# Rows of the experts gathered in quarters and turned by VectorE's 32x32 blocks instead of by TensorE

## The chip, the cores and the metric

The kernel runs on one core of one Trainium2 chip. The metric is the device time of one execution in microseconds (us), lower is better. One execution is also taken with the hardware profiler: its record (the trace) holds every instruction of the five engines, which are TensorE (PE, its weight loads apart as PEld), VectorE (DVE), ScalarE (ACT), GpSimd (POOL) and the queue processor SyncE (SP), and every DMA. Line numbers such as L1196 are those of the kernel before; in rows of the changed kernel they are its own.

## The reference: attention over a window, then one expert for each row

```python
def reference(q, k, v, w_gate, w_local, w1, w2):       # q, k, v: (8, 8, 576, 64)
    rel = pos[:, None] - pos[None, :]
    scores = where((rel >= 0) & (rel < 64), q @ k.T / 8, -1e9)
    x = (softmax(scores) @ v).transpose(0, 2, 1, 3).reshape(8, 576, 512)
    logits = x @ w_gate                                # 8 experts
    local = sigmoid(x @ w_local)
    for b in range(8):
        for s in range(576):
            fresh = argmax(logits[b, s])
            e = fresh if s == 0 or local[b, s] < 0.5 else prev
            prev = e
            p = softmax(logits[b, s])
            out[b, s] = p[e] * (relu(x[b, s] @ w1[e]) @ w2[e])   # w1: 512x1024, w2: 1024x512
```

## The kernel before: attention, a router and blocks of rows by expert

**Stages.** `attention` computes the 4608 rows of x in nine chunks of 512 and writes them to a table `xs` in DRAM, one row of 528 numbers for each row of x: 512 of x, and the row's weight p[e] sixteen times behind them (`Router.weigh`, L890). The `Router` finds each row's expert and sorts the rows by expert; `Router.table` (L945) makes the list of row numbers for every slot of 128 rows (`gx` to gather, `idx` to scatter) by small matmuls, once for the first three blocks during attention and once for the rest (`second`) while the first blocks run. Then `Experts.run` (L1474) works through 24 blocks, each of rows of one expert.

**Blocks.** A big block has two slots of 128 rows, a single (S) one, a half (H) 64 rows, a quarter (Q) 32 rows. `order` (L1498) is fixed: three first blocks (-1, -2, -3), then big 0, 1, S, 2, Q, 3, S, 4, 5, S, 6, Q, 7, S, 8, 9, H, 10, 11, 12, H. Big blocks are named by their number below. For a block, `rows` (L1144) issues one indirect DMA of GpSimd for each slot (128 row numbers, 128 rows of 2112 bytes), `weights` (L1170) loads 2 MB of w1 and 2 MB of w2 through SP's queue into a ring of four buffers. `turn` (L1189) makes x^T: four TensorE transposes of 128x128 into PSUM for each slot (L1196) and one copy to SBUF (L1197, VectorE in the blocks after the first three). A big block's two products are made by seven block products each instead of eight (`big_hidden` L1249, `big_result` L1302), from sums and differences that VectorE makes: of x^T and w1 in `prepare` (L1205: four of 128x256, four of 128x1024), of w2 in `prepare2` (L1238, four of 128x1024), of h in `halves` (L1243, four of 128x512).

**Order.** From the third block on, PE, SP, DVE and ACT issue in the order of the program text (`manual_schedule`); GpSimd's instructions are placed by the scheduler of the framework. In the text, iteration i issues: the gathers and weight loads of block i+2 (`fetch`), the hidden product of block i, `turn` and `prepare` of block i+1, the result of block i. On VectorE the three sums that finish y (L1327, "puts") therefore stand behind `turn` and `prepare` of the next block. The seventh product of a result reuses the PSUM buffer px that the second put reads. Two scatters per big block (L1394; the halves of its rows, y0 and y1) end it. A scatter waits until the scatter before it has landed, since both write `out`; y has two buffers, x six.

**A quarter** has its small products inside the result of the big block before it, and the block after it is turned and prepared in hooks of that result (L1550 to L1554).

Of the kernel before, what the change touches and what calls it, by code (L numbers as in the profile page):

```python
# [19 lines left out]
P = 128  # L20
# [15 lines left out]
PITCH = D + 16  # L36
# [6 lines left out]
FB = 3  # L43
# [40 lines left out]
def kernel(  # L84
# [12 lines left out]
    w1: bass.AP,  # L97
    w2: bass.AP,
# [7 lines left out]
    xs = dram.tile([N + 2, PITCH], F32, name="xs")  # L106
# [4 lines left out]
                gx=const.tile([P, NS], U32, name="gx"), gx1=const.tile([P, FIRST], U32, name="gx1"))  # L111
# [9 lines left out]
    moe = xs, w1, w2, out, tabs, lt, ident  # L121
    with ExitStack() as fast:
        ring = fast.enter_context(tc.tile_pool(name="ring", bufs=4))
        rt = Router(fast, tc, lt, xs, tabs, ident)
        ex = Experts(fast, tc, ring, *moe)
        zeros, n = ex.xp.tile([P, PITCH], F32, name="xg"), (ZR - T1) // HF
        nc.vector.memset(zeros[:HF], 0.0)
        for i in (ZR, N + 1):
            nc.gpsimd.dma_start(out=xs[i:i + 1, :], in_=zeros[:1])
        nc.gpsimd.dma_start(out=xs[T1:ZR, D:].rearrange("(c p) o -> p c o", p=HF),  # L130
                            in_=zeros[:HF, :n * (PITCH - D)].rearrange("p (c o) -> p c o", c=n))
        attention(tc, ring, kq, v3, v4, vt, vh, xs, lt, ok, wgs, wg2s, ident, rt, ex)
        ex.run(fast, rt, lambda ps: flag(nc, ps, ok, bad, tabs["ej"][:, NBLK:], rare, ident))
    if_rare = nc.values_load(rare[0:1, 0:1], min_val=0, max_val=1,  # L134
                             skip_runtime_bounds_check_because="the larger of two comparisons")
    with tc.If(if_rare > 0):
        if_bad = nc.values_load(bad[0:1, 0:1], min_val=0, max_val=1,
                                skip_runtime_bounds_check_because="the result of a comparison")
        with tc.If(if_bad > 0):
            careful(tc, q, k, v, xs, lt, wgs, ident)  # L140
# [27 lines left out]
def attention(ctx, tc, ring, kq, v3, v4, vt, vh, xs, lt, ok, wg, wg2, ident, rt, ex):  # L168
# [302 lines left out]
    for i, (sc, hp) in enumerate(units):  # L471
# [53 lines left out]
        if (sc, hp) == (NSC - 3, 3):  # L525
            ex.jobs = [ex.weights({}, -1, ("w1",), lambda: until(2, allr[:1, sc, hp, 0, :1]))]
            if side == ():
                ex.rows(ex.jobs[0], -1)
# [3 lines left out]
        if hp == HP - 1:  # L532
            if sc in GATED:
                nc.vector.tensor_reduce(lt[:, 4 * sc:4 * sc + 4, :], g.rearrange("p c h j e -> p c e (h j)"),
                                        axis=AX.X, op=Alu.add)
            nc.gpsimd.dma_start(out=xs[row_of(sc * SC):row_of(sc * SC) + SC, :D].rearrange("(c p) d -> p c d", p=P),
                                in_=x.rearrange("p c h j d -> p c (h j d)"))
# [11 lines left out]
def careful(ctx, tc, q, k, v, xs, lt, wgs, ident):  # L549
# [107 lines left out]
    def rows(st):  # L657
# [7 lines left out]
        nc.gpsimd.dma_start(out=xs[row_of(c * P):row_of(c * P) + P, :D], in_=x)  # L665
# [36 lines left out]
class Router:  # L702
# [9 lines left out]
    def __init__(self, ctx, tc, lt, xs, tabs, ident):  # L712
        self.nc, self.lt, self.xs, self.tabs, self.ident = tc.nc, lt, xs, tabs, ident
# [8 lines left out]
    def prepare(self):  # L722
# [17 lines left out]
        begin2 = tl("begin2", P, C)  # L740
# [4 lines left out]
        self.oh, self.rank = tl("oh", P, CV, E), tl("rank", P, CV, E)  # L745

# [5 lines left out]
        self.at = iota("posp", [P, 1], [[0, 1]], 1)  # L752
        self.cnt = [tl("cnt0", P, E), tl("cnt1", P, E)]
# [5 lines left out]
    def iota(self, name, shape, pattern, mul=0, base=0):  # L759
        i = self.tl(name + "_i", *shape, dt=I32)  # L760
        self.nc.gpsimd.iota(i, pattern=pattern, base=base, channel_multiplier=mul)
        f = self.tl(name, *shape)
        self.nc.vector.tensor_copy(f, i)
        return f
# [9 lines left out]
    def gate(self, part, psum):  # L774
# [111 lines left out]
        self.pt = tl("ptw", P, CMAX, PITCH - D)[:, :n]  # L886
        wide = [P, n, PITCH - D]
        vec.tensor_tensor(self.pt, last(pt).to_broadcast(wide), last(sm).to_broadcast(wide), op=Alu.mult)

    def weigh(self, part):  # L890

        chunks, xs = PART[part], self.xs
        c = chunks.start
        for a, b in ((0, T1), ) if not part else ((T1, ZR), (ZR, N)):
            for a, b in ((a, -(-a // P) * P), (-(-a // P) * P, b // P * P), (b // P * P, b)):
                if a >= b:
# [3 lines left out]
                    out=xs[row_of(a):row_of(a) + b - a, D:].rearrange("(c p) o -> p c o", p=p),  # L900
# [44 lines left out]
    def table(self, psum, cs, ns, lo, hi, idx, gx):  # L945

        nc, last, vec = self.nc, self.last, self.nc.vector
# [42 lines left out]
        else:  # L990
            vec.scalar_tensor_tensor(gx, at, float(ZR), at, Alu.is_ge, Alu.add)
# [139 lines left out]
class Experts:  # L1131


    def __init__(self, ctx, tc, ring, xs, w1, w2, out, tabs, lt, ident):
        self.tc, self.nc, self.ring = tc, tc.nc, ring
        self.xs, self.w1, self.w2, self.out, self.tabs, self.ident = xs, w1, w2, out, tabs, ident
        self.xp = ctx.enter_context(tc.tile_pool(name="ex_x", bufs=2))
        self.jobs = []
# [5 lines left out]
    def rows(self, st, n):  # L1144
# [13 lines left out]
        elif n >= KINDS[1]:  # L1158
            st.update(half=n - KINDS[1], rows=HF)
        for s in slots:  # L1160
            x = (self.xp if n == -1 else self.xq).tile([P, PITCH], F32, name="xg")
            asked = self.nc.gpsimd.indirect_dma_start(  # L1162
                out=x, out_offset=None, in_=self.xs[:rows, :],
                in_offset=bass.IndirectOffsetOnAxis(ap=gx[:, s:s + 1], axis=0))
            st["x"].append(x)
            st["asked"] = asked
        st["pw"] = [x[:, D:D + 1] for x in st["x"]]
        return st

    def weights(self, st, n, names=("w1", "w2"), behind=lambda: None):  # L1170
# [4 lines left out]
        for name, w, a, b in (("w1", self.w1, DK, F), ("w2", self.w2, FK, D)):  # L1175
# [13 lines left out]
    def turn(self, st, quiet, later=False):  # L1189
# [3 lines left out]
        for i, x in enumerate(st["x"]):  # L1193
            tp = self.ps_t.tile([P, DK, P], F32, name="tp")
            for kk in range(DK):
                nc.tensor.transpose(tp[:, kk, :n], x[a, kk * P:(kk + 1) * P], self.ident[a, a])  # L1196
            (nc.scalar.copy if quiet else nc.vector.tensor_copy)(xt[:, :, i * P:i * P + n], tp[:, :, :n])  # L1197
        if n < P:
            st["pw"] = pw = self.wk.tile([P, 1], F32, name="pw")
            for i in range(P // n):  # L1200
                nc.vector.tensor_copy(pw[i * n:(i + 1) * n], x[a, D:D + 1])
# [272 lines left out]
    def run(self, ctx, rt, last=None):  # L1474
# [44 lines left out]
        for i, n in enumerate(order):  # L1519
            quiet = i < FB  # L1520
            if i == FB - 1:
# [97 lines left out]
```

## Time and profile before

| | |
|---|---|
| time, median of 3 runs | 642.59 us (640.96 to 642.63) |
| the profiled execution | 642.1 us, of which the trace's span is 640.0 us |
| granted TensorE clock, mean | 0.994 |
| attention and router, to the first expert block | about 131 us (first transposes of L1196 at 131.2) |
| expert blocks | from there to the end |
| bytes moved by DMA | 166.43 MB, mean 260 GB/s |

The page gives busy time of each engine, a strip of the span in 40 slices, and groups of instructions by line. For this case the timeline, with the time at which each instruction starts and what ended the idle time ahead of it, says more: one block of the tail lasts 25 us, and the averages mix blocks of four kinds. Where a group stands with a mean duration, the time that one instruction takes from PE in a row of equal ones is shorter, since matmuls overlap; it is read from the start of the group to the start of the next.

### The profile page before, as it was taken

The page shows a single profiled execution, that of the slowest core. Times are in us where ns is not written, and L with a number is a line of the kernel's source. Part 1 is how long each engine was busy: PE and PEld are TensorE (multiplying, and loading weights), DVE is VectorE, ACT ScalarE, POOL GpSimd, SP SyncE. Part 2 cuts the span into 40 slices and gives each one's busy share as a digit, 9 for nine tenths or more (in the row PEclk, how much of TensorE's full clock was granted, in tenths as well). Part 3 has the DMA queues.
Part 4 walks back from the last instruction along what each step waited for, and adds up shares of the span by engine and source line. Part 5 has one row for each costly group of instructions (what it writes and reads, how often), then busy time and mean ns, then how long its engine had stood idle before and what let it go on. Part 6 is the DMA issues. An engine that isn't in the chain of part 4 may idle for free. (4 is left out here: it accounts for less than half of the span.)

```text
span 640.0 us, 14994 instructions
## 1 busy us (share of the span) xinstructions
PE 615.6 (96%) x6367; PEld 544.2 (85%) x6367; DVE 402.3 (63%) x752; ACT 200.6 (31%) x368; POOL 133.1 (21%) x132
## 2 busy tenths in 40 slices
PE   8889998899999999999999999999999999999995
PEld 7777777788889999978997999887997998899994
DVE  6676588879968775273654683362917752886730
ACT  3766765612572122113120312021211221213120
POOL 5422112430103202120302120211312022111101
PEclk9999998999999999999999999999999999999998
DMA  9999996969757645786958665769768556956501
GB/s 338 416 418 406 385 366 241 348 236 337 237 171 246 244 166 198 242 316 236 387 189 291 218 234 212 259 235 367 263 228 324 185 199 232 379 167 225 209 17 38
DMA packets 29318, 166.43 MB, mean 260 GB/s; under 512 B 8451, under 2 KB 9497, under 8 KB 20026
## 3 DMA queue, kind: packets, MB, share of 16 engines
q1 hardware_dynamic: 20394, 135.54, 58.4%
q0 software_dynamic: 8848, 29.85, 12.2%
q8 instruction: 52, 0.85, 0.5%
q14 instruction: 24, 0.20, 0.1%
HBM read 146.18 MB, written 19.59 MB: 259 GB/s over the span
## 5 line engine op out<-in xcount | busy, mean ns | idle before, releaser
L1394 POOL DMA_INDIRECT out_dram<-y,idx x36 | 41.1, 1141 | 339.1 <-DVE y L1327 196.5
L1318 PE MATMUL hp<-ws,hs 128*128 128x256 f32 x384 | 88.7, 380 | 0.0
L1318 PEld LDWEIGHTS hp<-ws,hs 128*128 128x128 f32 x384 | 72.6, 190 | 10.5 <-issue 0.8
L1268 PE MATMUL hp<-xs,ws 128*128 128x128 f32 x672 | 79.6, 275 | 0.0
L1268 PEld LDWEIGHTS hp<-xs,ws 128*128 128x128 f32 x672 | 77.3, 192 | 0.0
L1327 DVE SCALAR_TENSOR_TENSOR y<-hp,xg,kept 128x256 f32<-128x256 f32 x48 | 22.6, 482 | 74.2 <-issue 47.0
L1414 PE MATMUL hp<-xt,w 128*64 128x64 f32 (+2 forms) x640 | 66.2, 276 | 0.0
L1414 PEld LDWEIGHTS hp<-xt,w 128*128 128x128 f32 (+1 forms) x640 | 60.8, 170 | 4.1 <-issue 0.7
L1318 PE MATMUL hp<-w,h 128*128 128x256 f32 x256 | 61.1, 382 | 0.0
L1162 POOL DMA_INDIRECT xg<-xs,gx x40 | 50.3, 1258 | 45.6 <-issue 37.4
L1279 DVE TENSOR_TENSOR h<-hp,keep 128x512 f32<-128x512 f32 x42 | 28.6, 690 | 48.1 <-PE hp L1268 48.0
L1268 PEld LDWEIGHTS hp<-xt,w 128*128 128x128 f32 x448 | 53.2, 192 | 2.7 <-issue 1.3
L1268 PE MATMUL hp<-xt,w 128*128 128x128 f32 x448 | 54.7, 275 | 0.0
L1318 PEld LDWEIGHTS hp<-w,h 128*128 128x128 f32 x256 | 47.2, 190 | 6.3 <-issue 0.4
L431 PE MATMUL xo<-vb,p 128*64 128x74 f32 (+1 forms) x576 | 44.5, 230 | 7.0 <-issue 2.9
L416 ACT ACTIVATE p<-sp 128x512 f32<-128x512 f32 x72 | 39.2, 595 | 38.0 <-PE sp L385 35.9
L385 PEld LDWEIGHTS sp<-w 64*64 64x64 f32 x1296 | 38.7, 138 | 12.1 <-issue 8.5
L421 DVE TENSOR_TENSOR p<-p,mask 128x1024 f32<-128x1024 f32 x29 | 36.1, 1245 | 19.5 <-ACT p L416 19.3
L431 PEld LDWEIGHTS xo<-vb,p 128*64 128x64 f32 x576 | 38.9, 138 | 9.9 <-issue 4.4
L385 PE MATMUL sp<-w 64*64 64x128 f32 (+1 forms) x1296 | 43.8, 270 | 2.6 <-issue 1.5
L431 PE MATMUL xo<-va,p 128*64 128x74 f32 (+1 forms) x576 | 44.5, 230 | 1.2 <-issue 1.2
L1280 ACT ACTIVATE h<-h 128x512 f32<-128x512 f32 x42 | 26.3, 630 | 59.1 <-DVE h L1279 59.1
(280 smaller groups left out, 955.0 us busy)
## 6 DMA issues: line engine op xcount, KB each, us to landing
w<-in_w_dram SPq DMA_DIRECT2D x42, 2048.0 KB, 9.2
w<-in_kq_dram SPq DMA_DIRECT2D x17, 1024.0 KB, 8.7
w<-in_w_dram SPq DMA_DIRECT2D x24, 512.0 KB, 9.3
xs<-x POOLq DMA_DIRECT2D x9, 1024.0 KB, 9.5
va<-in_v_dram SPq DMA_DIRECT2D x5, 1184.0 KB, 8.9
vtt<-in_vt_dram SPq DMA_DIRECT2D x5, 1024.0 KB, 7.2
va<-in_v_dram SPq DMA_DIRECT2D x3, 1040.0 KB, 12.2
va<-in_v_dram SPq DMA_DIRECT2D x2, 520.0 KB, 6.8
```

Source lines behind the costliest of these rows:

```text
L385: nc.tensor.matmul(sp[j][c * WIN:(c + 1) * WIN, a:b], lhsT=kt[h, hp, block * WIN:(block + 1) * WIN], rhs=qt[h, hp, a:b], start=not biased, ...
L416: nc.scalar.activation(p[:, j], sp[j], Act.Exp, scale=DH ** -0.5)
L421: masked.append(nc.vector.tensor_tensor(p, p, m.to_broadcast([P, 2, SC]), op=Alu.mult))
L431: nc.tensor.matmul(xo[par * WIN:(par + 1) * WIN, j, s * VW:s * VW + n], lhsT=p[:, j, b * WIN:(b + 1) * WIN], rhs=w[:, s, 2 * hp + j, :n], ...
L1162: asked = self.nc.gpsimd.indirect_dma_start(out=x, out_offset=None, in_=self.xs[:rows, :], in_offset=bass.IndirectOffsetOnAxis(ap=gx[:, s: ...
L1268: nc.tensor.matmul(out[:, m, :], lhsT=a[:, kk, m * P:(m + 1) * P], rhs=b[:, kk, :], start=start and m + kk == 0, stop=stop and (m, kk) == ...
L1279: nc.vector.tensor_tensor(o, x, y, op=add)
L1280: nc.scalar.activation(o, x if y is None else o, Act.Relu)
L1318: nc.tensor.matmul(out, lhsT=a[:, m, :], rhs=b[:, m, :], start=start and m == 0, stop=stop and m == FK // 2 - 1, skip_group_check=True)
L1327: nc.vector.scalar_tensor_tensor(y[i][:, j * w:(j + 1) * w], x, pw[i], y2, Alu.mult, Alu.add)
L1394: self.nc.gpsimd.indirect_dma_start(out=self.out[:, :], out_offset=bass.IndirectOffsetOnAxis(ap=st["idx"][:, s:s + 1], axis=0), in_=y, in_ ...
L1414: nc.tensor.matmul(hp[a, i, :], lhsT=st["w1"][:, kk, m * P:(m + 1) * P][:, a], rhs=st["xt"][:, kk, :n], start=(kk == 0), stop=(kk == DK - 1))
```

## The change

- `xs` has rows of 512 numbers alone; the weights go to a table of their own, `xw`, with rows of 16.
- After the first four blocks, a slot is gathered as four sets of quarter rows (128 row numbers, 128 pieces of 512 bytes each): the set m brings, to partition 32a+r, quarter a of row 32m+r. VectorE then turns the slot with one instruction that transposes each 32x32 block. This gives x^T with its 512 numbers in another order, and w1 is laid out on the host in that order too (`w1t`). A half needs two sets and a quarter one. The first three blocks and big 0 are "plain": gathered and turned as before.
- The weights of a slot are gathered by one more indirect DMA each, behind those of the rows.
- The numbers of the quarters, g4 = 4 x row + a, are made at the end of the table by 16 matmuls with columns of the identity.
- From the third block on GpSimd's instructions are in program order too.
- In `Router.prepare` all iotas share one buffer.

```diff
@@ Router.prepare, Router.iota
+        group = self.tl("iota_i", P, P, dt=I32)[:, :1]
+        nc.gpsimd.iota(group, pattern=[[0, 1]], base=0, channel_multiplier=1)
+        nc.vector.tensor_scalar(group, group, QR.bit_length() - 1, None, Alu.arith_shift_right)
+        self.group = tl("group", P, 1)
+        nc.vector.tensor_copy(self.group, group)
...
-        i = self.tl(name + "_i", *shape, dt=I32)
+        i = self.tl("iota_i", P, P, dt=I32)[:shape[0], :n]
@@ Router.table
-            vec.scalar_tensor_tensor(gx, at, float(ZR), at, Alu.is_ge, Alu.add)
+            gf = t[:, 0]
+            vec.scalar_tensor_tensor(gf, at, float(ZR), at, Alu.is_ge, Alu.add)
+            vec.tensor_copy(gx, gf)
+            vec.tensor_scalar(gf, gf, 4.0, None, Alu.mult)
+            yield 1.0, True
+            places = psum()[:, :4 * ns].rearrange("p (m s) -> p m s", m=4)
+            for m in range(4):
+                for a in range(4):
+                    nc.tensor.matmul(places[a * QR:(a + 1) * QR, m], lhsT=self.ident[:, m * QR:(m + 1) * QR], rhs=gf,
+                                     start=True, stop=True)
+            vec.tensor_scalar(tabs["g4"], places, self.group, None, Alu.add)
@@ Experts.rows
+        st["plain"] = plain or n < 0
+        st["parts"] = range(2, 3) if "quarter" in st else range(st["rows"] // QR)
         for s in slots:
-            x = (self.xp if n == -1 else self.xq).tile([P, PITCH], F32, name="xg")
-            asked = self.nc.gpsimd.indirect_dma_start(
-                out=x, out_offset=None, in_=self.xs[:rows, :],
-                in_offset=bass.IndirectOffsetOnAxis(ap=gx[:, s:s + 1], axis=0))
+            x = (self.xp if n == -1 else self.xq).tile([P, D], F32, name="xg")
+            if st["plain"]:
+                st["asked"] = self.gather(x, self.xs, gx[:, s:s + 1], rows)
+            else:
+                quarter = self.xs.rearrange("n (i d) -> (n i) d", i=4)
+                for m in st["parts"]:
+                    st["asked"] = self.gather(x[:, m * P:(m + 1) * P], quarter, tabs["g4"][:, m, s:s + 1], 4 * rows)
             st["x"].append(x)
-            st["asked"] = asked
-        st["pw"] = [x[:, D:D + 1] for x in st["x"]]
+        for s in slots:
+            pw = (self.pws if n == -1 else self.xq).tile([P, PW], F32, name="pws")
+            self.gather(pw, self.xw, gx[:, s:s + 1], rows)
+            st["pw"].append(pw[:, :1])
@@ Experts.turn
+            if st["plain"]:
...
+                continue
+            first, parts = st["parts"][0], len(st["parts"])
+            nc.vector.transpose(
+                o[:, :, :n].rearrange("p j (m t) -> p m j t", m=parts),
+                x[:, first * P:(first + parts) * P].rearrange("p (m j d) -> p m j d", m=parts, j=DK))
@@ Experts.run
-                ctx.enter_context(tc.manual_schedule(engines={ET.PE, ET.SP, ET.DVE, ET.Activation}))
-                st = self.rows({}, order[FB])
-                with tc.issue_after(st["asked"].ins):
-                    jobs[i - 1].pop("later")()
+                ctx.enter_context(tc.manual_schedule(engines={ET.PE, ET.SP, ET.DVE, ET.Activation, ET.Pool}))
+                st = self.rows({}, order[FB], True)
+                jobs[i - 1].pop("later")()
@@ kernel
+        "w1t": i["moe_w1"].reshape(E, 4, DK, QR, F).transpose(0, 1, 3, 2, 4).reshape(E, P, DK * F),
```

**GpSimd, from the quarter behind big 6 to big 9, before.** L1385 is the scatter of the quarter, L1394 a scatter of 128 rows, L1162 a gather; the blocks come from the order above.

```order
L1385 DMA out_dram<-qy,idxq 18432x128
L1394 DMA out_dram<-y,idx 4608x512
L1162 DMA xg<-xs,gx 128x528 x2
L1394 DMA out_dram<-y,idx 4608x512 x2
L1162 DMA xg<-xs,gx 128x528 x2
L1394 DMA out_dram<-y,idx 4608x512 x2
```

The same stretch (big 6, Q, 7, S, 8) in the changed kernel, where L1429 is the quarter's scatter, L1438 a scatter and L1168 a gather (`xg` of quarter rows, `pws` of weights):

```order
L1429 DMA out_dram<-qy,idxq 18432x128
L1438 DMA out_dram<-y,idx 4608x512 x2
L1168 DMA xg<-xs,g_70 128x128 x4
L1168 DMA pws<-xw,gx 128x16
L1168 DMA xg<-xs,g_70 128x128 x8
L1168 DMA pws<-xw,gx 128x16 x2
L1438 DMA out_dram<-y,idx 4608x512 x2
L1168 DMA xg<-xs,g_70 128x128 x8
L1168 DMA pws<-xw,gx 128x16 x2
L1438 DMA out_dram<-y,idx 4608x512
```

Before, gathers follow the first scatter of big 6 and the second scatter comes behind them. In the changed kernel both scatters of big 6 come first, then fifteen gathers (those of S and of big 8), then both scatters of big 7, then ten gathers of big 9.

**VectorE at the turn from one big block to the next, before** (`hs` halves, `xt` the turned rows, `xs` the sums of x^T, `ws` those of w1, `y` the first put):

```order
L1220 TENSOR_TENSOR hs<-h,hs 128x512
L1197 COPY xt<-tp 128x4x128 x2
L1231 TENSOR_TENSOR xs<-xt 128x256
L1231 TENSOR_TENSOR xs<-xt,xs 128x256
L1231 TENSOR_TENSOR xs<-xt 128x256
```

and in the changed kernel:

```order
L1264 TENSOR_TENSOR hs<-h,hs 128x512
L1238 STREAM_TRANSPOSE xt<-xg 128x4x4x32 x2
L1275 TENSOR_TENSOR xs<-xt 128x256
L1275 TENSOR_TENSOR xs<-xt,xs 128x256
L1275 TENSOR_TENSOR xs<-xt 128x256
```

The transposing instruction takes the place of the copy and reads the gathered rows `xg` themselves, where the copy read TensorE's transposes in PSUM.

**TensorE ahead of the third block, in the changed kernel** (L991 the table's last matmuls, L165 the flag's transpose, L1312 the first product of the block):

```order
L991 LDWEIGHTS rowh
L991 MATMUL r<-colh,rowh 128x108
L1010 MATMUL r<-t,ident 32x54 x16
L165 MATMUL yp<-ident,ok 1x128
L1312 MATMUL hp<-xt,w 128x128 x8
```

The 16 matmuls L1010 stand between the table and the block; before, the flag's transpose (L161 there) followed the table at once.

More of the change, by code (lines that the diff above doesn't have):

```diff
@@ L119 @@
     bad, rare = const.tile([1, 1], I32, name="bad"), const.tile([1, 1], I32, name="rare")
-    moe = xs, w1, w2, out, tabs, lt, ident
+    xs = xs, xw
+    moe = xs, (w1, w1t), w2, out, tabs, lt, ident
     with ExitStack() as fast:
@@ L525, in attention @@
         if (sc, hp) == (NSC - 3, 3):
-            ex.jobs = [ex.weights({}, -1, ("w1",), lambda: until(2, allr[:1, sc, hp, 0, :1]))]
+            ex.jobs = [ex.weights({"plain": True}, -1, ("w1",), lambda: until(2, allr[:1, sc, hp, 0, :1]))]
             if side == ():
@@ L1142, in fetch, with gather, rows @@
         return self.weights(self.rows({}, n), n)
-    def rows(self, st, n):
+    def gather(self, out, table, idx, rows):
+        return self.nc.gpsimd.indirect_dma_start(
+            out=out, out_offset=None, in_=table[:rows, :],
+            in_offset=bass.IndirectOffsetOnAxis(ap=idx, axis=0))
+    def rows(self, st, n, plain=False):
         tabs = self.tabs
@@ L1174, in weights @@
         behind()
[L1175 removed]
+        for name, w, a, b in (("w1", self.w1[not st["plain"]], DK, F), ("w2", self.w2, FK, D)):
             if name not in names:
```

63 lines of the change are left out of this document (37 added, 26 removed).

## The prediction

> **What bounds the kernel now.** I read the page's busy shares first, then the timeline of one turn from a big block to the next, then GpSimd's own timeline in the tail.
>
> ```profile
> PE 615.6 (96%) x6367; PEld 544.2 (85%) x6367; DVE 402.3 (63%) x752; ACT 200.6 (31%) x368; POOL 133.1 (21%) x132
> ```
>
> TensorE is busy for 96% of the span, so a matmul taken from it is time saved, as long as nothing else becomes late. Whether something does is read from the turn between big 0 and big 1 (start, duration, engine, line):
>
> ```profile
> 203.98 1.04 PE L1196 MATMUL tp<-ident,xg 128*128 128x128 f32 x8
> 204.85 1.89 PE L1318 MATMUL hp<-w,h 128*128 128x256 f32 x8
> 206.32 1.28 DVE L1197 COPY xt<-tp 128x512 f32<-128x512 f32 x2
> ...
> 212.64 1.22 DVE L1220 TENSOR_TENSOR ws<-w,ws 128x1024 f32<-128x1024 f32 x1
> 213.77 0.87 DVE L1327 SCALAR_TENSOR_TENSOR y<-hp,xg,kept 128x256 f32<-128x256 f32 x2
> 215.21 1.89 PE L1318 MATMUL hp<-ws,h 128*128 128x256 f32 x8
> ...
> 216.94 1.28 PE L1268 MATMUL hp<-xt,w 128*128 128x128 f32 x10
> ```
>
> VectorE works without a gap from the halves of h to the second put, which ends at 213.77 + 0.87 = 214.64. The seventh result product reuses that put's PSUM buffer and starts at 215.21: VectorE has only 0.57 us in hand there. Whoever makes `turn` late, by rows that come late, makes the puts late, and TensorE with them.
>
> **What is removed.** Eight transposes of a big block take 204.85 - 203.98 = 0.87 us of TensorE.
>
> ```profile
> 528.00 0.46 PE L1196 MATMUL tp<-ident,xg 64*128 64x64 f32 x4
> 528.39 1.78 PE L1318 MATMUL hp<-w,h 128*128 128x256 f32 x7
> ...
> L1196 PE MATMUL tp<-ident,xg 128*128 128x128 f32 x144 | 19.1, 273 | 0.0
> ```
>
> The group counts 144 full transposes, 36 slots; the plain blocks (-1 to -3 and big 0) keep 8, and 28 slots lose theirs: 14 pairs x 0.87 = 12.2 us. A half's four take 528.39 - 528.00 = 0.39, and I give a quarter's four the same: 4 x 0.39 = 1.6. **Together -13.8 us.**
>
> **What is added on TensorE, the quarters' numbers.** They end the table, ahead of the first product of a block.
>
> ```profile
> 191.36 0.27 PE L161 MATMUL yp<-ident,ok 128*1 128x128 f32 x1
> 191.47 1.95 PE L1268 MATMUL hp<-xt,w 128*128 128x128 f32 x16
> 191.56 0.27 DVE L982 COPY t<-r 128x108 f32<-128x108 f32 x1 [2.00 <-PE r L980]
> 191.95 0.19 DVE L984 SCALAR_TENSOR_TENSOR at<-t 128x54 f32<-128x54 f32 x1
> ...
> L1381 PE MATMUL yp<-w,qt x64: 272/273/297, 303.2 to 304.9; 128*32 128x128 f32 x64
> ```
>
> Before, TensorE went on at 191.47 while VectorE worked the table out. Now its next instruction waits for the end of that chain: eight small VectorE instructions of 0.19 to 0.27, each on the one before, 8 x 0.25 = 2.0, and 0.2 each way between the engines (191.36 to 191.56): 2.4. The 16 matmuls have 32 columns of weights as L1381, whose 64 start 1.7 / 63 = 0.03 apart; the half's transposes start 0.1 apart. That is 0.5 to 1.6; I take 0.8, nearer to L1381. **+3.2** (2 to 4).
>
> **The shared iota buffer.**
>
> ```profile
> 43.95 0.17 DVE L733 MEMSET ones<- 128x128 f32 x1
> 44.19 0.32 POOL L735 TENSOR_SCALAR_AFFINE_SELECT tri<-ones 128x128 f32<-128x128 f32 x1 [1.18 <-DVE ones L733]
> ...
> PEld xo L431 <- DVE x L441: 2.7, 1, 2.7
> ```
>
> GpSimd made its iotas long ahead; now each must wait until VectorE has read the one before. One hand-over costs 0.07 (43.95 + 0.17 to 44.19) each way and an iota of about 0.2 to 0.3, eight or nine times: 3 to 4 us of VectorE's time in the attention's second chunk, where TensorE waits for VectorE's x once already, 2.7 us. Attention work stands between, so I pass on less than half: **+1.5** (0 to 3).
>
> **The start.** Two more fills of a table stand on GpSimd ahead of the masks:
>
> ```profile
> 3.02 1.03 POOL L129 DMA_DIRECT2D xs<-xg  x2
> ...
> 8.47 1.23 DVE L421 TENSOR_TENSOR p<-p,mask 128x1024 f32<-128x1024 f32 x1 [0.26 <-ACT p L416]
> ```
>
> They are about 0.5 each; the mask is needed at 8.47, where VectorE waits 0.26 for ScalarE anyway. **+0.3** (0 to 1).
>
> **The transposing instruction.** No row of before shows one. It stands where the copy stood and reads and writes the same 128x512, so I take the copy's 0.64 (1.28 for two). It is bounded by the 0.43 of a 128x256 and the 1.22 of a 128x1024 VectorE instruction (the 0.43 is half of the puts' 0.87). At 0.64 nothing changes on VectorE, but TensorE is now 0.87 earlier at the seventh product, against 0.57 in hand: it stalls 0.30 at each of the five turns from big to big (0-1, 4-5, 8-9, 10-11, 11-12): **+1.5** (0 by the lower bound, +7.3 by the upper, as 2 x 0.58 more each).
>
> The Trainium skill, "Vector Engine (DVE) Microarchitecture Reference", § 3.8, says the 32x32 transpose sustains one element per cycle and lane; with VectorE's 0.96 GHz of "VectorE: DVE Perf Modes" an estimate is 512 / 0.96 = 0.53 us. By that the stall of 0.30 is nearly gone and the sum 1.1 lower. No run here shows it yet.
>
> **What is moved: GpSimd.** Gathers go from 40 to 166, ten for each big block, and every one now stands behind both scatters of a block before. Rows of GpSimd unless DVE is named:
>
> ```profile
> L1162 POOL DMA_INDIRECT xg<-xs,gx x40 | 50.3, 1258 | 45.6 <-issue 37.4
> ...
> L1385 POOL DMA_INDIRECT out_dram<-qy,idxq x2 | 2.0, 1013 | 12.1 <-ACT qy L1384 12.1
> ...
> 451.19 1.00 POOL L1394 DMA_INDIRECT out_dram<-y,idx  x1 [7.78 <-DVE ws L1220]
> 452.50 1.95 POOL L1162 DMA_INDIRECT xg<-xs,gx  x1 [0.30 <-issue]
> 454.75 1.95 POOL L1162 DMA_INDIRECT xg<-xs,gx  x1 [0.30 <-issue]
> 459.53 1.01 POOL L1394 DMA_INDIRECT out_dram<-y,idx  x1 [2.82 <-DMA out_dram<-y,idx]
> 474.36 1.00 POOL L1394 DMA_INDIRECT out_dram<-y,idx  x1 [13.82 <-DVE y L1327]
> ...
> 482.99 1.01 POOL L1394 DMA_INDIRECT out_dram<-y,idx  x1 [5.05 <-DMA out_dram<-y,idx]
> ...
> 453.50 1.21 DVE L1220 TENSOR_TENSOR ws<-w,ws 128x1024 f32<-128x1024 f32 x1
> ...
> 541.21 0.97 POOL L1162 DMA_INDIRECT xg<-xs,gx  x1 [0.30 <-issue]
> 542.49 0.94 POOL L1162 DMA_INDIRECT xg<-xs,gx  x1 [0.30 <-issue]
> ...
> 493.99 1.22 DVE L1231 TENSOR_TENSOR ws<-w,ws 128x1024 f32<-128x1024 f32 x1
> ...
> 504.78 1.28 DVE L1197 COPY xt<-tp 128x512 f32<-128x512 f32 x2
> ...
> DMA to landing us min/median/max: 3.7/7.4/10.5
> ```
>
> A gather by itself comes every 542.49 - 541.21 = 1.28 us; while VectorE sums w1 (453.50) every 2.25. The quarter's scatter of short pieces costs 1.01 like the long ones, so I price a set of quarters as a gather. A second scatter starts 8.3 to 8.6 us behind the first, when that has landed.
>
> Take **big 9** (the order of GpSimd is in the section on the change). The second scatter of big 6 is at 459.53, so fifteen gathers run from 460.84 to 480.0. Only then goes the first scatter of big 7, ready since 474.36; the second follows 8.6 later, at 488.6, and the rows of big 9 start at 489.9, where before they stood ahead of it. Until 493.99 + 1.22 = 495.2 VectorE sums weights: three gathers at 2.25; the other five at 1.28, so the eighth starts at 501.6 and lands 7.4 later, at 509.0. VectorE wants the second slot at 504.78 + 0.64, less 1.3 for the transposes of S and big 8 that TensorE no longer makes: 504.1. **4.9 us late**; by the smallest landing time, 3.7, it would be 1.2, by the largest, 10.5, 8.0. **Big 5** (behind 3, S, 4) has the same order: 4.9.
>
> **Big 11** stands behind 9, H, 10:
>
> ```profile
> 548.47 1.69 POOL L1394 DMA_INDIRECT out_dram<-y,idx  x1 [5.04 <-DMA out_dram<-y,idx]
> ...
> 556.25 1.22 DVE L1231 TENSOR_TENSOR ws<-w,ws 128x1024 f32<-128x1024 f32 x1
> ...
> 564.13 1.28 DVE L1197 COPY xt<-tp 128x512 f32<-128x512 f32 x2
> ```
>
> Gathers from 550.5, three at 2.25 until the sums end at 557.5, five at 1.28: the eighth starts at 562.3 and lands at 569.7, wanted at 564.13 + 0.64 - 0.9 = 563.9: **5.8 late**. Behind the waiting transpose stand the sums of w1 and the puts, so TensorE waits as long. **Together +15.6** (0, if all are in time, to 25 by the largest landing time).
>
> The Trainium skill, "GPSIMD Engine Reference", § 1 Specifications, speaks against the change here: GpSimd shares its SBUF interfaces with VectorE and contends with VectorE instructions that have two SBUF inputs. The trace agrees: 1.95 against 0.97. If a gather of quarters escaped it, big 9, 5 and 11 would be 2.3, 2.3 and 2.8 late and the sum 642.2.
>
> **The sum.** The profiled execution took 642.1 (median of the runs 642.59): 642.1 - 13.8 + 3.2 + 1.5 + 0.3 + 1.5 + 15.6 = **650.4 us**. It stays PE-bound nearly everywhere; three waits take more than the transposes give.
>
> **Rivals.**
>
> - *GpSimd keeps up, faster.* If the eighth gather of big 5, 9 and 11 lands before VectorE asks for it, the 15.6 goes: 634.8 (632 to 640). It needs 5 to 6 us at each place: landings near 3.7, as pieces of 512 bytes carry a quarter of the bytes, and shorter waits between scatters. For it: 21% busy GpSimd, and 3.7 was seen. Against: scatters' waits alone take a third of a block.
> - *GpSimd bounds the whole tail, slower still.* At the group's mean, 1.26 + 0.31 = 1.57 a gather, a big block costs it ten gathers, 15.7, and 8.6 + 1.3 for its two scatters: 25.6, against a block's 216.94 - 191.47 = 25.5 less 0.87. Twelve big blocks, 1.0 us more each: 662. It decides where the mean gather exceeds about 1.5 with its gap. For it: VectorE is 63% busy and blocks GpSimd. Against: between the sums a gather takes 1.28.
> - *It cancels.* With half of the lateness (landing or contention less than priced), 640 to 644.
> - *A slow transposing instruction*, 1.22: 650.4 + 5.8 = 656, within the forecast's range.
>
> **Chances.** The forecast, late rows at three places, 644 to 657: 0.55. GpSimd keeps up: 0.25. Cancels: 0.08. GpSimd bounds all: 0.12. A measurement here tells about 0.3%, 1.9 us. Faster 0.25 and a part of the cancelling case, 0.27; same, 640.2 to 644.0, 0.10; slower 0.63. Both signs are likely, so the range reaches from the keeping-up case to the bound one, 633 to 663; the likeliest case alone has 644 to 657.
>
> **What would show it.** Right: VectorE idle ahead of its transpose L1238 at big 5, 9, 11, ended by a DMA of `xg`, some 5 us each; TensorE idle ahead of the seventh product there; GpSimd busy over 40%; a TensorE wait of 2 to 3 us ahead of L1010; L1238 near 0.64. Wrong: no idle time ahead of L1238, quarter sets far from 1 us, or landings near 3.7 throughout. Then the three terms fall, and the time goes to 635.

## The result, and the profile after

| | before | after |
|---|---|---|
| time, median of 18 runs each | 643.74 us (640.96 to 645.69) | 647.29 us (643.28 to 651.73) |
| ratio after / before | | 1.0058, 95% interval 1.0042 to 1.0075 |
| the profiled execution | 642.1 us, span 640.0 | 649.87 us, span 648.0 |

The change makes the kernel 0.58% slower, 3.6 us by the medians; 650.4 us was forecast, 8.3 more than the profiled execution of before. The profiled execution of the change is one of its slower ones and that of before one of its quicker ones, so the two profiles lie 8.0 us apart where the medians lie 3.6 apart: the profiles show where the time goes, and the medians how much it is. Below, the page of the changed kernel (line numbers are its own from here on):

```profile
span 648.0 us, 14959 instructions
...
PE 607.3 (94%) x6271; PEld 533.4 (82%) x6271; DVE 405.2 (63%) x757; ACT 200.5 (31%) x368; POOL 263.9 (41%) x261
...
PEclk9999999999998999999999999999999999979998
```

TensorE is busy for 8.3 us less, and yet the span is 8.0 us longer: its idle time went from 24.4 to 40.7 us. GpSimd's busy time doubled. The groups of the change, by shape (busy, mean ns | idle ahead of them, and what ended it):

```profile
L1168 POOL DMA_INDIRECT xg<-xs,g x118 | 126.6, 1073 | 36.0 <-issue 32.9 <-DMA xg<-xs,g 1.8 <-PE hp L1312 0.6
L1168 POOL DMA_INDIRECT pws<-xw,gx x40 | 44.6, 1115 | 12.2 <-issue 12.2
L1238 DVE STREAM_TRANSPOSE xt<-xg 128x512 f32<-128x512 f32 x28 | 18.5, 691 | 20.9 <-DMA xg<-xs,g 20.9
```

VectorE's transpose of a slot takes 0.69 us as recorded, 1.29 to 1.30 for two: the 1.28 of the two copies that it replaced. VectorE stood 20.9 us ahead of it for rows, at three places. The timeline of VectorE and TensorE at the last of them, where the rows of big 11 are turned inside the result of big 10:

```profile
562.84 0.70 DVE L1238 STREAM_TRANSPOSE xt<-xg 128x512 f32<-128x512 f32 x1
569.47 0.71 DVE L1238 STREAM_TRANSPOSE xt<-xg 128x512 f32<-128x512 f32 x1 [5.92 <-DMA xg<-xs,g]
...
575.29 1.22 DVE L1264 TENSOR_TENSOR ws<-w,ws 128x1024 f32<-128x1024 f32 x1
576.42 1.26 DVE L1371 SCALAR_TENSOR_TENSOR y<-hp,pws,kept 128x256 f32<-128x256 f32 x3
...
569.13 1.89 PE L1362 MATMUL hp<-w,hs 128*128 128x256 f32 x8
577.35 3.78 PE L1362 MATMUL hp<-ws,h 128*128 128x256 f32 x8 [6.33 <-DVE y L1371]
580.92 2.34 PE L1312 MATMUL hp<-xt,w 128*128 128x128 f32 x16
```

The second slot came 5.92 us late, the sums and puts behind it on VectorE moved with it, and TensorE stood 6.33 us ahead of the seventh product. Then it ran slowly: that product took 3.78 us where the same one takes 1.89 to 1.99 elsewhere. GpSimd's rows say why the slot was late (scatters L1438, gathers L1168):

```profile
539.76 1.02 POOL L1438 DMA_INDIRECT out_dram<-y,idx  x1 [1.88 <-DVE y L1371]
550.40 1.78 POOL L1438 DMA_INDIRECT out_dram<-y,idx  x1 [9.62 <-ACT y L1489]
552.49 1.95 POOL L1168 DMA_INDIRECT xg<-xs,g  x1 [0.30 <-issue]
...
563.44 0.95 POOL L1168 DMA_INDIRECT xg<-xs,g  x1 [0.30 <-issue]
```

The eight sets of quarters start behind the second scatter of big 9 and the last one starts at 563.44, as VectorE ends the first slot (562.84 + 0.70 = 563.54).

**Where the 8.0 us lie**, from the starts of the same products in both timelines (first product of the first expert block, of the third, of big 0; the result of the last half; the end of the span):

| stretch | before | after | difference | forecast |
|---|---|---|---|---|
| start to the first expert block | 133.41 | 135.68 | +2.27 | +1.8 |
| to the third block's first product (the table) | 58.06 | 61.65 | +3.6 | +3.2 |
| to big 0's first product | 25.47 | 26.48 | +1.0 | 0 |
| to the result of the last half | 412.33 | 411.11 | -1.2 | +3.3 |
| to the end of the span | 10.73 | 13.08 | +2.35 | 0 |

The first row is the spread from one execution to the next (experiments 1 and 12). Cut at the start of each block's products, the fourth stretch is -14.3 us where transposes went, and +13.1 us at nine places: 8.35 at big 11, 0.81 and 0.63 at the S behind big 3 and big 7, 0.55 to 0.57 at four turns from a big block to a big block, 0.51 and 0.53 at the quarters.

### The profile page after: what moved, and what is told of

It is laid out like the page before. It is cut to its first block, busy times and chain, and to the rows that moved or that the text cites. A ratio compares the mean times of both kernels' runs of the same rounds, so it can differ in the third digit from the quotient of the medians.

```text
span 648.0 us, 14959 instructions
## 1 busy us (share of the span) xinstructions
PE 607.3 (94%) x6271; PEld 533.4 (82%) x6271; DVE 405.2 (63%) x757; ACT 200.5 (31%) x368; POOL 263.9 (41%) x261
## 5 line engine op out<-in xcount | busy, mean ns | idle before, releaser
L1168 POOL DMA_INDIRECT xg<-xs,g x118 | 126.6, 1073 | 36.0 <-issue 32.9
L1438 POOL DMA_INDIRECT out_dram<-y,idx x36 | 40.8, 1132 | 214.3 <-DVE y L1371 91.9
L1312 PE MATMUL hp<-xs,ws 128*128 128x128 f32 x672 | 79.6, 275 | 0.0
L1312 PEld LDWEIGHTS hp<-xs,ws 128*128 128x128 f32 x672 | 77.3, 192 | 0.0
L1312 PEld LDWEIGHTS hp<-xt,w 128*128 128x128 f32 x448 | 54.8, 197 | 2.8 <-issue 1.8
L1312 PE MATMUL hp<-xt,w 128*128 128x128 f32 x448 | 56.1, 279 | 0.0
L1371 DVE SCALAR_TENSOR_TENSOR y<-hp,pws,kept 128x256 f32<-128x256 f32 x48 | 21.7, 478 | 51.0 <-issue 34.9
L1168 POOL DMA_INDIRECT pws<-xw,gx x40 | 44.6, 1115 | 12.2 <-issue 12.2
L425 DVE TENSOR_TENSOR p<-p,mask 128x1024 f32<-128x1024 f32 x29 | 37.9, 1311 | 18.0 <-ACT p L420 17.8
L1275 DVE TENSOR_TENSOR ws<-w 128x1024 f32<-128x1024 f32 x32 | 38.9, 1219 | 11.4 <-PE hp L1362 11.4
## 6 DMA issues: line engine op xcount, KB each, us to landing
xs<-x POOLq DMA_DIRECT2D x9, 1024.0 KB, 10.1
va<-in_v_dram SPq DMA_DIRECT2D x3, 1040.0 KB, 13.7
```

The costliest lines, as they stand in the source:

```text
L425: masked.append(nc.vector.tensor_tensor(p, p, m.to_broadcast([P, 2, SC]), op=Alu.mult))
L1168: return self.nc.gpsimd.indirect_dma_start(out=out, out_offset=None, in_=table[:rows, :], in_offset=bass.IndirectOffsetOnAxis(ap=idx, axis=0))
L1275: self.nc.vector.tensor_tensor(o, x, y, op=sub)
L1312: nc.tensor.matmul(out[:, m, :], lhsT=a[:, kk, m * P:(m + 1) * P], rhs=b[:, kk, :], start=start and m + kk == 0, stop=stop and (m, kk) == ...
L1371: nc.vector.scalar_tensor_tensor(y[i][:, j * w:(j + 1) * w], x, pw[i], y2, Alu.mult, Alu.add)
L1438: self.nc.gpsimd.indirect_dma_start(out=self.out[:, :], out_offset=bass.IndirectOffsetOnAxis(ap=st["idx"][:, s:s + 1], axis=0), in_=y, in_ ...
```

## The experiments

They were made in three sets, each on a chip of its own with the kernel before beside it: 1 to 4 (642.84 us for the kernel before), 5 to 8 (643.75) and 9 to 12 (645.33). Ratios are to the kernel before of the same set, with a 95% interval. Edits are against the changed kernel.

**1. The changed kernel again.**

> The changed kernel once more, without an edit, as the ground for the three runs beside it. In its first profile VectorE's transposes waited for rows three times, 7.57 and 7.40 us (the S behind big 3 and big 7) and 5.92 us (big 11), and TensorE stood 6.33 us ahead of the seventh product beside the last. If these waits come from the order on GpSimd, all three are there again, within 2 us; if they come from chance in the landing of single DMAs, they move to other blocks or go. Time 647 us (644 to 651).

648.33 us, ratio 1.0095 (1.0076 to 1.0114). VectorE waited for rows at the same three places, 20.2 us in all, and TensorE again stood at big 11:

```profile
573.91 3.78 PE L1362 MATMUL hp<-ws,h 128*128 128x256 f32 x8 [6.34 <-DVE y L1371]
```

The waits are not chance; that the order makes them, experiment 2 shows. The start was chance: its first expert block began at 132.8, 2.9 us sooner than in the first profile.

**2. Rows one block earlier.** Iteration i issues the gathers of block i+3 ahead of its own two scatters, where the change issues them at the start of iteration i+1, behind these.

```diff
             self.turn(jobs[i + 1], i + 1 < FB)
+            if i + 1 >= FB and i + 3 < len(order):
+                self.ahead[order[i + 3]] = self.rows({}, order[i + 3])
...
-        return self.weights(self.rows({}, n), n)
+        return self.weights(self.ahead.pop(n, None) or self.rows({}, n), n)
...
-            pw = (self.pws if n == -1 else self.xq).tile([P, PW], F32, name="pws")
+            pw = (self.pws.tile([P, PW], F32, name="pws") if n == -1 else
+                  self.xq.tile([P, PW], F32, name="pws", bufs=8))
```

> The gathers of a block are issued one block earlier, ahead of the two scatters of the block that is then worked on, and no longer behind them; their number is the same. If the order on GpSimd makes the rows late (the theory), VectorE's transposes no longer wait, TensorE no longer stands at big 11, and the time falls by 5 to 8 us against the changed kernel, to 639 to 642. If the number of gathers does it (ten to a big block, up to 2 us each beside VectorE's sums), the waits stay within a few us somewhere and the time falls by less than 2 us.

638.19 us, ratio 0.9931 (0.9908 to 0.9953): 10.1 us less than the run beside it, more than expected. The transposes no longer wait, though the gathers are as many and a little longer:

```profile
L1168 POOL DMA_INDIRECT xg<-xs,g x118 | 130.1, 1103 | 36.0 <-issue 34.7 <-PE hp L1313 0.3 <-DMA xg<-xs,g 0.3
...
L1239 DVE STREAM_TRANSPOSE xt<-xg 128x512 f32<-128x512 f32 x28 | 18.4, 688 | 0.0
```

At big 11 the loss falls from 8.36 to 0.58 us, at the two S from 0.49 and 0.23 to nothing. By the profiles the fourth stretch is 9.5 us shorter (401.69 against 411.23); the order on GpSimd, with so many gathers in it, was the whole cost of the late rows. The eight buffers for the weights of the rows (`pws`) only let them be held longer: in the changed kernel the gathers of weights never waited for a buffer (all of the 12.2 us ahead of them is "issue").

**3. The quarters' numbers later.** The matmuls and the last VectorE instruction go behind the first piece of the third block's hidden product, and the gathers that need them behind that product.

```diff
-            yield 1.0, True
-            places = psum()[:, :4 * ns].rearrange("p (m s) -> p m s", m=4)
...
+            def numbers():
+                places = psum()[:, :4 * ns].rearrange("p (m s) -> p m s", m=4)
...
+            self.numbers = [numbers]
...
+                make = (lambda: rt.numbers.pop()() if rt.numbers else None) if i == FB - 1 else step
...
+            if i == FB - 1:
+                make()
+                jobs.append(self.fetch(order[i + 2]))
```

> The 16 matmuls of the quarters' numbers are issued behind the first piece of the third block's hidden product, so that TensorE does not stand for VectorE's chain ahead of it; the gathers that need them are issued behind that hidden product. Theory: the wait of 2.5 us and the matmuls cost 3.6 us, and a further 1.0 us went because TensorE's first 16 matmuls after the wait ran slowly (2.96 us for 1.95); without the wait both go, but for the matmuls' 0.9: 3.5 to 4.5 us less than the changed kernel. Rival: the slow matmuls have another cause; then 2.5 us less and they stay slow.

644.55 us, ratio 1.0024 (1.0003 to 1.0044), 3.8 us less than the run beside it. TensorE goes from the table straight into the block (both timelines, TensorE; first the changed kernel of experiment 1):

```profile
193.40 0.59 PE L1010 MATMUL r<-t,ident 128*32 128x54 f32 x32 [2.48 <-DVE t L1005]
193.92 0.27 PE L165 MATMUL yp<-ident,ok 128*1 128x128 f32 x1
194.02 3.27 PE L1312 MATMUL hp<-xt,w 128*128 128x128 f32 x16
```

```profile
192.73 1.95 PE L1315 MATMUL hp<-xt,w 128*128 128x128 f32 x16
194.51 1.95 PE L1315 MATMUL hp<-xs,ws 128*128 128x128 f32 x16
196.40 0.59 PE L1011 MATMUL r<-t,ident 128*32 128x54 f32 x32
```

The stretch to the third block's product loses nothing (58.07 against 58.06 before; 61.22 in the run beside it). The matmuls themselves, recorded as 32, push what follows by 0.5 us (196.40 to 196.91), and the first 16 matmuls of the block are back at 1.95 us. This doesn't show that the wait alone made them slow: in experiment 2 they took 1.95 us behind the same wait.

**4. The fills behind the masks.** The five DMAs into the spare rows of `xs` and `xw` become a function that attention calls later.

```diff
-        for i in (ZR, N + 1):
-            nc.gpsimd.dma_start(out=xs[0][i:i + 1, :], in_=zeros[:1])
...
+        rt.fill = fill
...
+        if i == 3 * HP:
+            rt.fill()
```

> The DMAs that fill the spare rows of the two tables are issued behind the masks on GpSimd and not ahead of them; the shared iota buffer stays. Theory: the two more fills ahead of the masks are what delays attention by 2.3 us (the first mask came 0.95 us later, and the third weight load waits for it), so the first block's hidden product starts 2 us or more earlier than in the changed kernel, and the time falls by about 2 to 3 us. Rival (the step of the prediction): the shared iota buffer costs it; then the first expert block starts within 0.5 us of the changed kernel and the time is the same.

647.06 us, ratio 1.0081 (1.0059 to 1.0103), 1.3 us under the run beside it with intervals that overlap. The first expert block began at 132.9, against 132.8 beside it without the edit, not sooner as expected. VectorE's first x came 0.8 us sooner (14.36 against 15.19), but by the end of attention nothing is left of that. With the spread that experiment 12 shows, one profile each can't show a difference of 2 us here.

**5. Both edits that helped.**

> Both edits that helped: rows gathered one block earlier, and the quarters' numbers behind the first product of the third block. If the wait at big 11 and the stand ahead of the third block are separate costs, they add: 638.2 - 3.8 = 634.4 us (633 to 636). If the earlier gathers already hide part of the later start, 636 or more.

635.74 us, ratio 0.9889 (0.9867 to 0.9910), on the second chip. Against 2, by the ratios, 0.42% or 2.7 us, where 3.8 were expected; they add at least in the main.

**6. Own iotas, on top of 5.** Each iota gets a place in memory that the router fills only later.

```diff
-        i = self.tl("iota_i", P, P, dt=I32)[:shape[0], :n]
+        i = self.place(n)[:shape[0]]
```

> The same with a place of its own for each iota (in memory that the router does not use yet), so that GpSimd makes them long ahead again. If the shared buffer costs attention what the prediction gave it, 1.5 us less than the run without this edit (1 to 2.5); if attention waits for its DMAs there anyway, within 0.7 us of it.

636.17 us, ratio 0.9882 (0.9860 to 0.9904), against 635.74: the shared buffer costs nothing that can be measured.

**7. The fourth sum of w1 behind the puts, on top of 5.**

```diff
+            if rest is not None and o is s4:
+                rest["rest"] = lambda o=o, x=x, y=y, op=op: self.nc.vector.tensor_tensor(o, x, y, op=op)
+                break
...
-            hooks = (step, ) * 6
+            hooks = (step, ) * 5 + (jobs[i + 1].get("rest", step), )
```

> The same two edits, and at the turns from a big block to a big block the fourth sum of w1 stands behind the three puts of y on VectorE, not ahead of them. Theory: the stall of 0.3 us ahead of the seventh product, with the weight load behind it, is what costs 0.55 us at each such turn; the sum takes 1.2 us, so the puts end in time and 5 x 0.55 = 2.7 us go. Rival: the 0.55 us have another source (the next block's first matmuls wait for something else); then less than 1 us goes.

633.56 us, ratio 0.9853 (0.9826 to 0.9880): 2.2 us less than 5, with intervals that overlap at their ends, so the traces have to decide. At each of the five turns 0.55 to 0.64 us become 0.00 to 0.01; the put now ends ahead of the matmul that waits for its buffer (TensorE's wait is gone, and the sum fills VectorE's gap behind the puts):

```profile
240.82 0.87 DVE L1378 SCALAR_TENSOR_TENSOR y<-hp,pws,kept 128x256 f32<-128x256 f32 x2
...
242.43 1.89 PE L1369 MATMUL hp<-ws,h 128*128 128x256 f32 x8
...
242.70 0.48 DVE L1378 SCALAR_TENSOR_TENSOR y<-hp,pws,kept 128x256 f32<-128x256 f32 x1 [1.01 <-PE hp L1369]
243.10 1.22 DVE L1269 TENSOR_TENSOR ws<-w,ws 128x1024 f32<-128x1024 f32 x1
```

This is the fastest kernel of the study, 1.5% under the kernel before.

**8. Whole rows and TensorE's transposes in the changed order.** `st["plain"] = True` for every block; the numbers, the weights' gathers and GpSimd's order stay.

> The changed kernel with GpSimd in program order, the quarters' numbers and the weights' own gathers, but every block gathered in whole rows and transposed on TensorE: four gathers to a big block and not ten. If the order alone makes the rows of big 11 late, VectorE or TensorE waits for them here too, some us. If order and number do it together (the theory), its rows land at about 562, before they are needed, nothing waits there, and the time is that of before plus the table's 3.2 us and what attention loses: 646 to 649 us.

655.49 us, ratio 1.0193 (1.0166 to 1.0221): slower than both, and not the 646 to 649 expected. Big 11 loses nothing here (0.01), as expected with four gathers. But TensorE itself now waits for the rows of the S behind big 3 and big 7:

```profile
PE tp L1234 <- DMA xg<-xs,gx: 10.8, 2, 9.2
```

At the first of these places 9.76 us went, and 2.22 us in the product behind it; at the second 1.74. The profiled execution took 663.87 us, where the other four took 654.87 to 656.29, so the size of the first wait may be that of this one execution. That the rows are late is not: the gather of this S is issued at 329.81, behind both scatters of big 3, and TensorE stands for it from 330.49 on, while no gather of the changed kernel, of those whose landing its trace holds, landed sooner than 2.4 us after its issue. So the order alone, with few gathers, makes the rows of an S late; by how much is open. In the changed kernel the same lateness (7.57 and 7.40 us) falls on VectorE, which has no sums to make for an S, and cost TensorE 0.8 and 0.6.

**9. Whole rows and TensorE's transposes in the order of 7.**

> The run with the three edits (633.56 us), with whole rows gathered and transposed on TensorE again: what the turning on VectorE is worth when no rows are late. By the prediction's first term 13.8 us less the 1.0 us that the quarters' waits give back: 633.6 + 12.8 = 646.4 us (645 to 648). If 86 gathers fewer give something back (VectorE's sums and the weight loads no longer beside them), the difference is under 10 us.

656.83 us, ratio 1.0178 (1.0148 to 1.0208), on the third chip: 10 us more than expected. From big 0 to the last half it takes 412.50 us, where kernel 7 takes 398.85 and the kernel before 412.33: by these profiles turning on VectorE is worth 13.65 us when no rows are late. Kernel 7 ran on another chip, and on this one the kernel before took 414.23 us for the stretch (experiment 12), so some 2 us of the 13.65 are within the spread. The time as a whole holds 4.8 us more in the third block's result, for which see 10 and 11, and at the end of the span 4.4 us more than kernel 7 (16.79 against 12.38).

**10 and 11. The quarter's pieces one product later, on top of 7; the sums of w1 ahead of the turning.**

```diff
-                hooks = one, turned, two, (lambda: None), (lambda: self.turn(after, False, True)), \
+                hooks = (lambda: None), one, turned, two, (lambda: self.turn(after, False, True)), \
```

> The three edits that helped (rows one block earlier, numbers later, fourth sum behind the puts), and the three pieces of a quarter stand one product later in the result that they are put into. TensorE waits 0.5 us there at each of the two quarters, because VectorE turns the quarter's rows too late; one product is 1.7 us, so both waits go: 633.6 - 1.0 = 632.6 us (631.5 to 633.6). If the waits only move to the quarter's later pieces, the time is the same.

```diff
+        if st["fast1"] and not quiet and not later:
+            self.sums1(st)
         st["xt"] = xt = self.xtp.tile([P, DK, BIG], F32, name="xt")
...
+    def sums1(self, st):
         w = quarters(st["w1"], DK, F)
```

> The changed kernel, with VectorE's four sums of w1 ahead of the turning of the rows and not behind it; GpSimd's order stays. The rows of big 11 are then wanted 4.6 us later. If late rows are what TensorE waits for (the theory), the 6.3 us ahead of the seventh product there shrink to 1 to 2 us, and the time falls by 4 to 6.5 us against the 648.3 us of the changed kernel beside it; the S waits stay. If VectorE's work itself were too long there, nothing changes.

725.81 us (ratio 1.1251, 1.1197 to 1.1305) and 732.03 us (1.1390, 1.1326 to 1.1453): neither question is answered. Long before the first quarter, in the third block's result, ScalarE and TensorE stand in kernel 10 for something that the profile cannot name ("remote", "issue"):

```profile
224.30 0.47 ACT L1374 ACTIVATE kept<-hp,pws 128x256 f32<-128x256 f32 x1 [13.69 <-remote]
224.83 3.78 PE L1369 MATMUL hp<-ws,hs 128*128 128x256 f32 x8 [12.87 <-issue]
```

Kernel 9, on the same chip, stands at the same place in the same way, for less:

```profile
213.49 0.84 ACT L1374 ACTIVATE kept<-hp,pws 128x256 f32<-128x256 f32 x2 [3.75 <-remote]
```

In kernel 11 ScalarE stands in this way from 193.1 to 202.8 us, ahead of its first instruction of the third block. From the third block on such waits of ScalarE add up to 96 us in kernel 10, 81 in 11 and 7 in 9 (those above 0.8 us), about what the times are longer in 10 and 11. The kernel before on that chip shows nothing of it, nor do the kernels of the other two sets. Kernels 9, 10 and 11 have different edits, which speaks for the chip and against the edits; but neither the changed kernel nor kernel 7 ran there, so it stays open whether these kernels too would be 80 us or more slower on that chip. It wasn't tried, and the gain of kernel 7 is shown on one chip alone.

**12. The kernel before again.**

> The kernel before, without an edit, for a second profile. In eight profiles of the changed kernel and its variants, whose attention is the same but for the fills and the iotas, the first expert block's product began at 132.8 to 135.7 us; in the one profile of before at 133.4. If attention loses by the change, as the prediction has it (1.8 us), it begins at 133.5 or earlier here; if those numbers are the spread of one execution to the next, anywhere in 132.8 to 135.7.

646.71 us in one run. Its first expert block began at 135.56, in the profile of before at 133.41; in the twelve of the changed kernel and its variants between 132.8 and 135.68. The spread is that of one execution to the next, and no loss of attention can be shown. The end of the span is another matter: from the last half's result 11.16 us here and 10.73 before, 12.35 to 13.31 in the first profile of the change and in 1 to 7, 14.74 and 16.79 in 8 and 9. In all of them the last scatter starts 4.42 to 4.48 us behind that result, so the difference lies wholly behind the last scatter, where the profile shows no engine at work.

## Why the prediction was right, and where not

**The direction and the kind of mechanism** held: rows that come late behind the scatters on GpSimd and the matmuls of the quarters' numbers take what the transposes give. The size did not: the forecast was 1.3% slower, and the medians are 0.58% apart, 3.6 us of 8.3. That the profiled execution, 649.87 us, fell on the forecast of 650.4 is luck: from big 0 to the last half it is 4.5 us better than forecast, and the start (0.5 us), the table (0.4), the third block (1.0) and the end (2.35) make up for that. Of the signs named, the wait ahead of L1010 (2.47 us), the transposing instruction (0.69 us) and GpSimd's 41% came; VectorE's wait for rows came at one of the three blocks named.

**Transposes, -13.8:** right. -14.3 us in the places where they went (13.7 to 14.7 in 1 to 7), and 13.65 by 9 against 7. For the quarters the term had the wrong sign: 0.39 us of transposes go, but TensorE then waits 0.84 to 0.87 us for VectorE, so each loses 0.5 us.

**The quarters' numbers, +3.2:** right, 3.2 to 3.6, and 2.5 of it the wait. What was missed is TensorE's slow start behind the wait, up to 1.6 us more, which some of the profiles have and others not.

**Big to big, +1.5:** the mechanism right, the size half: TensorE's wait is 0.28 to 0.30 as forecast, but a turn loses 0.55 to 0.57, since the weight load of the seventh product waits too (0.68 us at the first turn). Experiment 7 shows that it is VectorE's order. (The rows quoted there for the turn from big 0 to big 1 were those of the turn from the third block to big 0; the next turns have the same form.)

**Late rows, +15.6:** the step that was mis-sized; 9.8 us were lost to late rows in the profile. Big 11 was forecast at 5.8 and VectorE waited 5.92, for which TensorE lost 8.35. Big 5 and big 9 were forecast at 4.9 each and VectorE did not wait. For big 9, GpSimd and then VectorE:

```profile
481.44 1.02 POOL L1438 DMA_INDIRECT out_dram<-y,idx  x1 [0.30 <-issue]
485.50 1.01 POOL L1438 DMA_INDIRECT out_dram<-y,idx  x1 [3.03 <-issue]
486.81 0.99 POOL L1168 DMA_INDIRECT xg<-xs,g  x1 [0.30 <-issue]
...
498.17 0.94 POOL L1168 DMA_INDIRECT xg<-xs,g  x1 [0.30 <-issue]
...
505.57 1.29 DVE L1238 STREAM_TRANSPOSE xt<-xg 128x512 f32<-128x512 f32 x2
```

The first scatter of big 7 went at 481.44, near the 480.0 that was worked out. But the second followed after 4.06 us, not 8.6, so the eighth gather began 3.4 us sooner than forecast, at 498.17. It also landed sooner: 2.5 us behind its issue, at 500.7, where the median of 7.4 had been taken. And VectorE asked for the second slot at 506.2, not at 504.1. So the rows of big 9 had 5.5 us in hand; with VectorE asking at 506.2, either of the first two alone would have sufficed. (A slip of 0.2 us in the sum, 501.6 for 501.8, plays no part.) At big 5 the eighth gather landed at 369.1, and the second slot was asked for at 372.8. The stretches between two scatters, first one in the kernel before, then two in the changed one (length, busy times, clock, DMA share, GB/s):

```profile
474.40:483.00 8.60, 8.60 (x76) 8.52 (x75) 0.60 (x1) 1.07 (x2) 2.94 (x4) 1.00 0.92 335
```

```profile
481.40:485.50 4.10, 4.10 (x28) 3.21 (x27) 1.45 (x3) 0.00 (x0) 1.02 (x2) 1.00 0.67 190
452.60:460.80 8.20, 8.20 (x76) 8.20 (x76) 8.14 (x8) 1.76 (x3) 1.00 (x1) 1.00 0.66 258
```

The 8.6 came from a stretch in which the DMA engines were busy for 0.92 and moved 335 GB/s. The fifteen gathers pushed the first scatter to a later stretch with 0.67 and 190 GB/s, where it landed in half the time. Durations, this one and the landing of a gather, were carried along with a step that itself had moved to another moment; that was the error. What makes a scatter land sooner isn't shown: the scatters of big 6 in the changed kernel lie 8.2 us apart at a share of 0.66, so the share of busy DMA engines alone doesn't decide it. In their place came two that the prediction did not name, the S behind big 3 and big 7 (+1.4 us). At big 11 the slow clock behind the wait added 1.8 us.

**The shared iotas and the fills, +1.8:** not shown. Experiments 4 and 6 gain nothing that can be measured.

**The end, 0 in the forecast:** 1.2 to 2.6 us more in those profiles. It lies behind the last scatter, nothing in the profile names it, and it was not taken apart.

**The rivals.** "GpSimd keeps up" was priced at 634.8 us. Experiment 2, in which the rows are in time, came to 638.2. "GpSimd bounds the whole tail" was wrong: between the sums a gather takes 0.94 us and 0.30 behind it, and ten fit into a block. "A slow transposing instruction" was wrong: 0.69 us. The median of 647.29 lies in the lower part of the range given for late rows at three places (644 to 657).

## What to carry to other kernels

A queue that is put in program order makes each of its steps wait for all ahead of it: before work is moved onto it, write out for each consumer what stands ahead of its data there, and place what must arrive early ahead of what may wait (here the gathers of a block moved ahead of two scatters, 10 us). The price of lateness is set by the engine on which it falls and by what is queued behind: a wait of 7.6 us cost 0.8 where VectorE had no sums to make, one of 5.9 us cost 8.4 where sums and puts stood behind it, and one of 9.2 us on TensorE itself, in one execution of kernel 8, cost 12. An edit that takes work from the bound engine also takes the slack of the others; look at the next wait at once.

## What the runs showed of the hardware

TensorE can pay twice for a stand. Behind 6.33 us, eight matmuls of 256 columns took 3.78 us for 1.89, at a granted clock of 0.50 (the changed kernel's stretches: length, busy times of PE to POOL, clock, DMA share, GB/s):

```profile
577.30:581.20 3.90, 3.85 (x10) 3.14 (x11) 0.42 (x2) 0.00 (x0) 2.85 (x4) 0.50 0.44 150
581.20:585.00 3.80, 3.80 (x34) 3.80 (x34) 3.77 (x4) 1.06 (x2) 2.87 (x2) 0.93 0.05 4
```

The Trainium skill, "TensorE: Matmul & The Clock Gate", What's actually happening, has half the rate after an idle window of about 3.4 us and full rate after as much busy time; the trace agrees here, half the clock for nearly 3.9 us. A shorter stand isn't safe: behind one of only 2.5 us ahead of the third block the first 16 matmuls took 2.96 and 3.27 us for 1.95 in the two profiles of the changed kernel, at a granted clock of 0.62 and 0.56 as they ran, and 1.95 at a clock of 1.00 in that of experiment 2 with the same stand. What decides between the two isn't shown.
